# v loaded as bf16 from the GpSimd queue, and clock-sized dummy matmuls, in a fused linear-attention and feed-forward kernel

## The chip, the cores and the metric

The kernel runs on one core of one Trainium2 chip. The time is the device time of one execution in microseconds (us), and less is better. Quoted times are medians over the executions of a comparison; a run counts as slow when it is over 1.5% above the fastest of the same kernel, else as fast. Slow runs stand in the medians, but not in the ratios. The granted clock is the share of TensorE's full clock that the chip let through. The engines in the profile lines are PE (TensorE), ACT (ScalarE), DVE (VectorE), POOL (GpSimd) and SP (SyncE, which only issues DMAs here). A cast is an elementwise multiply by a decay table that also turns float32 into bf16; in this kernel most casts of q and k run on GpSimd, all the arithmetic between the two large matmuls on ScalarE and VectorE.

## The reference

Attention with a decay per head, worked out block by block with a carried state, and then two matmuls with a smooth clipped function between them.

```python
# q, k, v: (4, 8, 768, 64) float32; w_in: (512, 2048); w_out: (2048, 512); output (3072, 512)
for b in range(nb):                                   # blocks of 64 positions
    intra = einsum('bhic,bhjc->bhij', qb, kb) * Dmask[None]
    intra = einsum('bhij,bhjd->bhid', intra, vb)
    inter = einsum('bhid,bhde->bhie', qb * lam_pow[None], kv_state)
    out[:, :, sl] = intra + inter
    kv_state = lam_block * kv_state + einsum('bhsd,bhse->bhde', kb * rev_pow, vb)
# ...
h = x @ w_in                                          # x: attention output, (3072, 512)
g = where(h >= 1, h, where(h <= -1, 0, (h + 1)**2 / 4))
return g @ w_out
```

## The kernel before

The attention goes over the tokens in 12 pairs of 128-token chunks ("pair m" below, 0 to 11). For each pair q, k and v are loaded, 512 KB each in float32, by three DMAs from the SP queue. The weights are loaded by eight DMAs from GpSimd, which cast them to bf16 on the way (512 KB each as written): four blocks of w_in, four of w_out.

```python
# loads of one pair: x = 0 is q, 1 is k, 2 is v
t = ld.tile([128, H, 2, D], F32, name=f"x{x}f", tag=f"x{x}f")
i = (k, v)[x - 1][b, :, s0:s0 + 2 * C, :].rearrange("h (j e) d -> j h (e d)", e=2)
d = nc.sync.dma_start(out=t.rearrange("p h e d -> p h (e d)"), in_=i)
# ... (and then, for v, one cast for each chunk)
nc.scalar.copy(out=v_sb[c % NV], in_=qkv_ld[c, 2])
# casts of k and q; eng is VectorE for a few early chunks, else GpSimd
eng.tensor_tensor(ho(ks[c])[:, bs], hs(qkv_ld[c, 1])[:, bs], ho(_bc(tab, 2, D))[:, bs], op=AX.mult)
# between the two large matmuls, on VectorE, once for each 128x1024 piece
nc.vector.tensor_scalar(t, r, 0.5, 1.0, op0=AX.mult, op1=AX.min)
nc.vector.tensor_tensor(w, r, t, op=AX.subtract)
nc.vector.tensor_tensor(gT[s][...], w[...], t[...], op=AX.mult)
```

The order of the instructions on each engine is worked out when the kernel is built, by a planner in the kernel: each operation has a duration, needs, and a due time, and an engine takes the ready operation that is due first. Where an operation needs an earlier one on the same engine, the planner counts from the earlier one's issue, not from the end of its transfer, unless the need is entered as `gate`:

```python
ready[u.eng].append((max(y.t if y.eng == u.eng and y.key != u.gate else y.end + ...
# a weight load enters its wait as a gate
add(("w",) + it, "POOL", 900, lambda it=it, wait=gated: f_w(it, wait), need, due=pos_ * 1e-3, dma=2560)
if key is not None:
    OPS[("w",) + it].gate = key
```

While PE has nothing to do at the start, dummy matmuls (the planner's `warm`) fill it; they are meant to bring its clock up and to keep it there. In the trace of this kernel they start 0.213 us apart from 4.17 to 8.2 us and 0.109 us apart from 8.37 on; the first clock record, full clock, begins at 8.32 (the page counts the time before it as full).

## Time and profile before

| | before |
|---|---|
| median of 3 (lowest to highest) | 221.37 us (221.31 to 224.28) |
| span of the profiled execution, granted clock | 217.8 us, 0.997 |
| PE streaming of real work, without dummies | 181.0 us |
| first matmul with w_in, with w_out | 19.29 us, 40.73 us |
| ScalarE casts of v | 24, together 14.9 us |

The prediction below shows the page's main lines. Three more views are needed later. First, GpSimd by time; columns are start, length, engine, line, operation and tiles, count, and in brackets the idle time before it and what ended it.

```profile
23.74 1.55 POOL L167 DMA_DIRECT2D w_out_sb<-in_moe_w_out_dram  x2 [7.75 <-DMA w_in_sb<-in_moe_w_in_dram]
27.95 1.28 POOL L300 TENSOR_TENSOR qs<-x0f,tab_q 128x512 bf16<-128x512 f32 x1 [2.66 <-DMA x0f<-in_q_dram]
30.78 1.04 POOL L292 TENSOR_TENSOR ks<-x1f,tab_p 128x512 bf16<-128x512 f32 x1 [1.55 <-DMA x1f<-in_k_dram]
```

The two w_out loads go as soon as the third w_in block is there (23.45 us). Second, GpSimd and VectorE where both are busy:

```profile
47.34 2.42 POOL L292 TENSOR_TENSOR ks<-x1f,tab_p 128x512 bf16<-128x512 f32 x2 [4.99 <-DMA x1f<-in_k_dram]
```

### The profile page before, as it was taken

What the parts mean: (1) busy time and instruction counts of PE and PEld (TensorE: products, weight loads), DVE (VectorE), ACT (ScalarE), POOL (GpSimd) and SP (SyncE); (2) the same over time, 40 slices, a digit from 0 to 9 for tenths busy, and PEclk for the clock granted to TensorE, in tenths of its full rate; (3) what the DMA queues carried; (4) which work ended last, traced back from release to release, by engine and by line L of the source; (5) the groups of instructions that cost most, each with busy time, mean ns of one, the idle gap of its engine ahead of it and who ended that gap; (6) DMA issues with size and microseconds to landing.
All of it is one profiled execution on the core that took longest, in us unless ns stands there. A gap on an engine that the chain in (4) does not pass through costs nothing.

```text
span 217.8 us, 5513 instructions
## 1 busy us (share of the span) xinstructions
PE 206.8 (95%) x2343; PEld 120.9 (55%) x2343; DVE 148.6 (68%) x235; ACT 115.4 (53%) x200; POOL 60.2 (28%) x63
## 2 busy tenths in 40 slices
PE   3999878999999999999999999999999999999993
PEld 2777667557546767766654454544544444444442
DVE  4585975799980899899899769668467455454301
ACT  3257667427617867396557556564634643555020
POOL 5390242337382662366263421000000000000000
PEclk9999999999999999999999999999999999999998
DMA  6999999999899999999999966211011101110022
GB/s 168 290 236 196 252 235 192 203 282 176 227 236 245 219 258 170 263 230 266 181 286 207 272 192 163 38 53 48 0 51 48 43 8 48 48 48 16 35 96 96
DMA packets 64586, 34.43 MB, mean 158 GB/s; under 512 B 20402, under 2 KB 61618, under 8 KB 64562
## 3 DMA queue, kind: packets, MB, share of 16 engines
q1 hardware_dynamic: 60336, 29.89, 61.5%
q0 software_dynamic: 4224, 4.19, 11.9%
q8 instruction: 18, 0.29, 0.6%
q14 instruction: 6, 0.05, 0.1%
q10 hardware_dynamic: 2, 0.00, 0.0%
HBM read 27.26 MB, written 6.29 MB: 154 GB/s over the span
## 4 chain that ended last, share of the span: by engine, by line
PE 79%; DMA 15%; SPq 2%; ACT 1%; DVE 1%; issue 1%
PE py L487 36%; PE ph L439 34%; DMA x2f<-in_v_dram 9%; DMA x0f<-in_q_dram 3%; DMA w_in_sb<-in_moe_w_in_dram 3%; PE px L388 3%; PE ps L360 2%; PE px L372 2%; PE py L481 1%; SPq L557 1%; PE ps L401 1%; DVE sc L421 1%; ACT r L448 1%; ACT xT L428 0%; PE pt L360 0%
## 5 line engine op out<-in xcount | busy, mean ns | idle before, releaser
L439 PE MATMUL ph<-xT,w_in_sb 128*128 128x256 bf16 (+1 forms) x576 | 95.8, 308 | 2.6 <-ACT xT L428 1.1
L448 ACT ACTIVATE r<-ph,one 128x512 bf16<-128x512 f32 x96 | 65.6, 688 | 51.9 <-PE ph L439 43.7
L487 PE MATMUL py<-w_out_sb,gT 128*128 128x512 bf16 x368 | 90.6, 380 | 0.0
L439 PEld LDWEIGHTS <-w_in_sb 128*128 128x128 bf16 x576 | 54.9, 98 | 32.7 <-issue 2.1
L487 PEld LDWEIGHTS <-gT 128*128 128x128 bf16 x368 | 34.4, 98 | 38.0
L458 DVE TENSOR_SCALAR t<-r 128x1024 bf16<-128x1024 bf16 x48 | 27.6, 575 | 21.7 <-ACT r L448 21.7
L464 DVE TENSOR_TENSOR w<-r,t 128x1024 bf16<-128x1024 bf16 x48 | 40.1, 835 | 1.3
L469 DVE TENSOR_TENSOR gT<-w,t 128x1024 bf16<-128x1024 bf16 x48 | 37.7, 785 | 1.3
L300 POOL TENSOR_TENSOR qs<-x0f,tab_q 128x512 bf16<-128x512 f32 (+1 forms) x22 | 26.1, 1204 | 43.7 <-DMA x0f<-in_q_dram 33.7
L292 POOL TENSOR_TENSOR ks<-x1f,tab_p 128x512 bf16<-128x512 f32 (+1 forms) x20 | 25.4, 1285 | 14.2 <-DMA x1f<-in_k_dram 9.0
L421 DVE TENSOR_TENSOR sc<-ps,causal 128x512 bf16<-128x512 f32 x23 | 15.8, 689 | 12.4 <-PE pt L360 11.0
L492 ACT COPY osb<-py 128x512 f32<-128x512 f32 x23 | 13.5, 587 | 16.5 <-PE py L487 15.5
L428 ACT CAST xT<-px 128x512 bf16<-128x512 f32 x24 | 13.1, 587 | 13.0 <-PE px L388 9.1
L421 DVE TENSOR_TENSOR sc<-pt,causal 128x512 bf16<-128x512 f32 x22 | 14.9, 679 | 0.0
L315 ACT CAST v<-x2f 128x512 bf16<-128x512 f32 x24 | 13.8, 621 | 1.1 <-DMA x2f<-in_v_dram 1.1
L274 PE MATMUL ph<-ident 128*128 128x256 bf16 x68 | 10.8, 315 | 0.0
L360 PE MATMUL ps<-qT,kT 64*64 64x128 bf16 x184 | 10.6, 220 | 0.0
L360 PEld LDWEIGHTS <-kT 64*64 64x64 bf16 x384 | 7.7, 106 | 4.3 <-issue 4.0
L416 ACT CAST ub<-state 128x256 bf16<-128x256 f32 x19 | 7.7, 405 | 4.0 <-DVE state L407 2.0
L360 PE MATMUL pt<-qT,kT 64*64 64x128 bf16 x176 | 9.7, 219 | 0.0
L409 DVE TENSOR_TENSOR state<-state,ps 128x256 f32<-128x256 f32 x8 | 3.3, 416 | 7.8 <-PE pt L401 6.9
L388 PEld LDWEIGHTS <-v 64*64 64x64 bf16 x384 | 5.8, 106 | 4.7 <-issue 4.7
(59 smaller groups left out, 89.0 us busy)
## 6 DMA issues: line engine op xcount, KB each, us to landing
x0f<-in_q_dram SPq DMA_DIRECT2D x12, 512.0 KB, 5.8
x1f<-in_k_dram SPq DMA_DIRECT2D x12, 512.0 KB, 6.8
x2f<-in_v_dram SPq DMA_DIRECT2D x12, 512.0 KB, 7.2
out_dram<-osb SPq DMA_DIRECT2D x23, 256.0 KB, 2.1
w_in_sb<-in_moe_w_in_dram POOLq DMA_DIRECT2D x4, 512.0 KB, 8.7
w_out_sb<-in_moe_w_out_dram POOLq DMA_DIRECT2D x4, 512.0 KB, 10.8
kT<-ks SPq DMA_TRANSPOSE x18, 4.1
out_dram<-osb SPq DMA_DIRECT2D x1, 192.0 KB, 1.9
```

The lines of the kernel that those rows point to most:

```text
L292: eng.tensor_tensor(ho(ks[c])[:, bs], hs(qkv_ld[c, 1])[:, bs], ho(_bc(tab, 2, D))[:, bs], op=AX.mult)
L300: eng.tensor_tensor(ho(qs[m, e])[:, bs], hs(qkv_ld[m, 0][:, :, e])[:, bs], ho(_bc(tab_q[:, e, m % (NCB // 2), :], 2, D))[:, bs], op=AX.mult)
L315: nc.scalar.copy(out=v_sb[c % NV], in_=qkv_ld[c, 2])
L360: nc.tensor.matmul(pst[a, r][HD[i], b, :], lhsT=kT[a][HD[r], b, HD[i]], rhs=q_cols(2 * m + i, b, HD[r]), start=True, stop=True)
L421: nc.vector.tensor_tensor(sc_sb[c][:, g], pst[c, g], _bc(causal2[:, c % 2], 1, HP), op=AX.mult)
L439: nc.tensor.matmul(ph[:, j * m:(j + 1) * m], lhsT=w_in_sb[:, ko, (ni + j) * 128:(ni + j + 1) * 128], rhs=xT[s][:, ko, tok], start=(ko == 0 ...
L448: nc.scalar.activation(out=o, in_=x, func=AF.Relu, bias=one[:, 0:1])
L458: nc.vector.tensor_scalar(t, r, 0.5, 1.0, op0=AX.mult, op1=AX.min)
L464: nc.vector.tensor_tensor(w, r, t, op=AX.subtract)
L469: nc.vector.tensor_tensor(gT[s][:, f - RW * n:f, tok].rearrange("p (a b) m -> p a b m", a=RW), w.rearrange("p a (b m) -> p a b m", m=m), t ...
L487: nc.tensor.matmul(py_t[s, ms], lhsT=gT[s][:, ko, ms * 128:(ms + 1) * 128], rhs=w_out_sb[:, ko, :], start=(ko == 0), stop=(ko == FO - 1))
L492: nc.scalar.copy(out=osb[s, ms], in_=py_t[s, ms])
```

## The change

The intent is to take v's casts off ScalarE, and its loads off the SP queue, by letting a GpSimd DMA write bf16 directly. The dummy matmuls are counted at the clock that they run at (213 ns each instead of 107), so that they no longer delay the first transposes.

```diff
+    def f_loadv(m, wait):
+        i = v[b, :, s0:s0 + 2 * C, :].rearrange("h (j e) d -> j h (e d)", e=2)
+        d = nc.gpsimd.dma_start(out=v_sb[m % NV].rearrange("p h e d -> p h (e d)"), in_=i)
+        if wait is not None:
+            tc.add_manual_dep(d.ins, ld_dma[wait] if isinstance(wait, tuple) else w_dma[wait].ins.name, SYNC)
...
-    def cast_v(c):
-        nc.scalar.copy(out=v_sb[c % NV], in_=qkv_ld[c, 2])
...
+    GATE_V = {2: 3, 3: 5}     # v(2) waits for w_in block 3, v(3) for w_out block 1 (counted from 0)
...
+                add(("lv", m), "POOL", 3400 if m == 0 else VNS, ... lambda m=m, g=g: f_loadv(m, g),
+                    [key, ("C", m - NV), ("C", m - 1 - NV), ("u", m - NV)], due=pos_ * 1e-3 if m < EARLY else od - LDV, dma=VDMA)
...
-    EARLY = 3
+    EARLY = 6                 # loads of pairs below this are due at once
...
-    WARM = (2700, 18000, 107, 0.8)
+    WARM = (4200, 18000, 213, 0.8, 8300)
```

Left out here: v(0) is issued early in the set-up, pair 3 comes after the w_out blocks in the order, its q and k loads wait for one w_out block more, several leads of the planner are larger (q and k are cast and transposed further ahead), pair 4 joins the merged matmul groups, and a few k casts move between VectorE and GpSimd.

More of the change, by code (lines that the diff above doesn't have):

```diff
@@ L65 @@
     W_IN = (4, 4, 4, 4)
-    MERGED = tuple(range(5,12))
+    MERGED = tuple(range(4,12))
     SWITCH = 96
     W_OF = [i for i, n in enumerate(W_IN) for _ in range(n)]
-    ORDER = [0, 1, (0, 0), (0, 1), (0, 2), (0, 3), 2, (1, 0), (1, 1), 3, (1, 2), (1, 3)]
-    D0 = (8350, 10000, 15450, 17000)
+    ORDER = [0, 1, (0, 0), (0, 1), (0, 2), (0, 3), 2, (1, 0), (1, 1), (1, 2), (1, 3), 3]
+    D0 = (8350, 10000, 15450, 15000)
     FIRST = [(0, 2), (2, 4)]
     L0 = [(0, 0), (0, 1), (0, 2), (0, 3), (1, 0), (1, 1), (1, 2), (1, 3)]
-    GATE = {(0, 0): ('lq', 1), 2: 0, (1, 0): 2, 3: 4, (1, 2): 4}
+    GATE = {(0, 0): ('lq', 1), 2: 0, (1, 0): 2, 3: 5, (1, 2): 4}
     LORD = {}
+    GATE_V = {2: 3, 3: 5}
+    VNS, VDMA = 1800, 1350
+    LDV = 20000
+    GEN = 1350, 1800
     DBG = False
@@ L104 @@
     SYNC = mybir.DependencyInfo(mybir.DependencyClass.Sync, mybir.DependencyReason.DATA)
+    NUB, NV = 4, 4
+    v_sb = [const.tile([128, H, 2, D], BF16, name=f"v{i}") for i in range(NV)]
+    def f_loadv(m, wait):
+        b, s0 = m // (NCB // 2), 2 * (m % (NCB // 2)) * C
+        i = v[b, :, s0:s0 + 2 * C, :].rearrange("h (j e) d -> j h (e d)", e=2)
+        d = nc.gpsimd.dma_start(out=v_sb[m % NV].rearrange("p h e d -> p h (e d)"), in_=i)
+        ld_dma["lv", m] = d.ins.name
+        if wait is not None:
+            tc.add_manual_dep(d.ins, ld_dma[wait] if isinstance(wait, tuple) else w_dma[wait].ins.name, SYNC)
     nc.scalar.preload_act_table_set("natural_log_exp_and_others")
@@ L114 @@
     make_identity(nc, ident)
+    f_loadv(0, None)
     causal2 = const.tile([128, 2, 128], F32)
@@ L121 @@
                 base=base, pattern=[[1, 2], [2, 64]], channel_multiplier=-2)
-    NUB, NV = 4, 4
     ub = [const.tile([128, HP, D], BF16, name=f"ub{i}") for i in range(NUB)]
-    v_sb = [const.tile([128, H, D], BF16, name=f"v{i}") for i in range(NV)]
     state = const.tile([128, HP, D], F32)
@@ L188 @@
     LDD, STD = 16000, 3000
-    QXD, KXD = 7000, 7000
-    AD, BD = (8000, 4000), (4000, 2000)
-    UD, TD = (9000, 9000), (8000, 8000)
-    KT_ACT = (1,)
-    K_DVE = (0,1,2,3,5)
-    ON_DVE = ((0,0),(0,1),(2,1))
-    SHARED = (1,(0,1))
-    W_AFTER = {1: ("cq", 1, 0)}
+    QXD, KXD = 12000, 10000
+    AD, BD = (7000, 7000), (3000, 3500)
+    UD, TD = (12000, 9000), (12000, 8000)
+    KT_ACT = (1,3)
+    K_DVE = (0,2,3)
+    ON_DVE = ((0,0),(0,1))
+    SHARED = ()
+    W_AFTER = {1: ("cq", 1, 1)}
     def run_plan(free):
@@ L222, in run_plan @@
                 ready[x.eng].append((0, x))
-        out_seq, xfer, dma_free, fetched = [], [0] * RING, FIRST_BYTE, 0
+        out_seq, xfer, dma_free, fetched, hw_free = [], [0] * RING, FIRST_BYTE, 0, FIRST_BYTE
         while len(out_seq) < len(ops):
@@ L237, in run_plan @@
             if x.dma:
-                dma_free = max(dma_free, t + (1300 if e == "SP" else 2100)) + x.dma
-                x.end = dma_free + (400 if x.key[0] in ("lk", "lv", "lq") and x.key[1] < CPS // 2 else 1000 if x.key[:2] == ("w", 0) else 1400)
+                hw = x.key[0] in ("lk", "lq")
+                dma_free = max(dma_free, t + (1300 if e == "SP" else 2100)) + (GEN[0] if hw else x.dma)
+                if hw:
+                    hw_free = max(hw_free, t + 1300) + GEN[1]
+                x.end = max(dma_free, hw_free if hw else 0) + (400 if x.key[0] in ("lk", "lq") and x.key[1] < CPS // 2 else 1000 if x.key[:2] == ("w", 0) or x.key[0] == "lv" else 1400)
                 if x.key[0] in ("lk", "lv", "lq") and x.key[1] >= FAR // 2:
@@ L252, in run_plan @@
                 n = int((t - pe_end - 50) * WARM[3] / WARM[2])
+                w = 256 if t < WARM[4] else 512
                 if t > WARM[1]:
@@ L258, in run_plan @@
                         print(f"{t / 1e3:9.3f} 0 WARM {n} {x.key}")
-                    warm(max(n, 0))
+                    warm(max(n, 0), w)
                     if x.key in (("s", 1), ("C", 0)):
@@ L264, in run_plan, with warm @@
             x.fn()
-    WARM = (2700, 18000, 107, 0.8)
+    WARM = (4200, 18000, 213, 0.8, 8300)
     hot = [None]
-    def warm(n):
+    def warm(n, w):
         for _ in range(n):
@@ L273, in warm @@
                 hot[0] = pp_h.tile([128, MS], F32, name="ph", tag="ph")
-            nc.tensor.matmul(hot[0][:, :256], lhsT=ident, rhs=_bc(ident, 1, 2), start=True, stop=True)
+            nc.tensor.matmul(hot[0][:, :w], lhsT=ident, rhs=_bc(ident, 1, w // 128), start=True, stop=True)
     def mm(*cols):
@@ L387, in f_c @@
                     c, (r, b, _) = 2 * m + i, place(2 * j + g)
-                    nc.tensor.matmul(px[HD[g], i, j, :], lhsT=v_sb[(2 * m + e) % NV][HD[i], 2 * j + g, :],
+                    nc.tensor.matmul(px[HD[g], i, j, :], lhsT=v_sb[m % NV][HD[i], 2 * j + g, e, :],
                                      rhs=sc_sb[2 * m + e][HD[i], r, b, :],
@@ L401, in f_u @@
                         nc.tensor.matmul(pu[i][HD[r], b, :], lhsT=ks[2 * m + e][HD[i], 2 * b + r, :],
-                                         rhs=v_sb[(2 * m + e) % NV][HD[i], 4 * r + b, :],
+                                         rhs=v_sb[m % NV][HD[i], 4 * r + b, e, :],
                                          start=(e == 0 and b == 0), stop=True, skip_group_check=True)
@@ L512 @@
     T0, STEP = 22000, 1075
-    LEAD, APART = 6000, 3000
-    PARTS = {1: 2, 2: 2, 4: 1}
-    EARLY = 3
+    LEAD, APART = 2000, 3000
+    PARTS = {1: 2, 2: 2, 3: 2, 4: 1}
+    EARLY = 6
     parts = {s: [slice(p * MS // n, (p + 1) * MS // n) for p in range(n)] for s in range(NST) for n in (PARTS.get(s, 1),)}
@@ L554, in f_load @@
         else:
-            t = ld.tile([128, H, 2, D], F32, name=f"x{x}f", tag=f"x{x}f")
-            i = (k, v)[x - 1][b, :, s0:s0 + 2 * C, :].rearrange("h (j e) d -> j h (e d)", e=2)
+            t = ld.tile([128, H, 2, D], F32, name="x1f", tag="x1f")
+            i = k[b, :, s0:s0 + 2 * C, :].rearrange("h (j e) d -> j h (e d)", e=2)
             d = nc.sync.dma_start(out=t.rearrange("p h e d -> p h (e d)"), in_=i)
@@ L582 @@
             add(("w",) + it, "POOL", 900, lambda it=it, wait=gated: f_w(it, wait), need, due=pos_ * 1e-3,
-                dma=2560)
+                dma=2600)
             if key is not None:
@@ L591 @@
         for x in LORD.get(m, (0, 1, 2)):
+            if x == 2:
+                g = GATE_V.get(m)
+                key = None if g is None else g if isinstance(g, tuple) else ("w",) + w_seen[g]
+                add(("lv", m), "POOL", 3400 if m == 0 else VNS, (lambda: None) if m == 0 else lambda m=m, g=g: f_loadv(m, g),
+                    [key, ("C", m - NV), ("C", m - 1 - NV), ("u", m - NV)], due=pos_ * 1e-3 if m < EARLY else od - LDV, dma=VDMA)
+                pos_ += 1
+                continue
             need = [("w",) + w_seen[gated] if gated is not None else ("w",) + w_seen[-2] if len(w_seen) > 1 else None]
-            need += [[("cq", m - LQ, 0), ("cq", m - LQ, 1), ("cq", m - LQ, 9)], [("cast", 2 * (m - LD) + 1, 1), ("cast", 2 * (m - LD) + 1, 9)],
-                     [("cast", 2 * (m - LD) + 1, 2)]][x]
+            need += [[("cq", m - LQ, 0), ("cq", m - LQ, 1), ("cq", m - LQ, 9)], [("cast", 2 * (m - LD) + 1, 1), ("cast", 2 * (m - LD) + 1, 9)]][x]
             add(("lq lk lv".split()[x], m), "SP", 700, lambda m=m, x=x, wait=gated: f_load(2 * m, x, wait), need,
@@ L611 @@
                 [("lk", m), ("cast", c - 1, 1), ("t", c - NQK), u_op(m - NQK // 2)])
-            add(("cast", c, 2), "ACT", 640, lambda c=c: cast_v(c), [("lv", m), ("C", m - NV // 2), u_op(m - NV // 2), ("cast", c - 1, 2)])
         for i in range(2):
@@ L637 @@
                 add(("t", c), "SP", 1200, lambda c=c: f_kx(c), [("cast", c, 1), ("m", c - NQT, 1)], due=od - KXD, dma=640)
-        u_need = lambda m: [x for c in (2 * m, 2 * m + 1) for x in (("cast", c, 9), ("cast", c, 1), ("cast", c, 2))] + \
+        u_need = lambda m: [x for c in (2 * m, 2 * m + 1) for x in (("cast", c, 9), ("cast", c, 1))] + [("lv", m)] + \
             [("sum", 2 * m - 1 if m % (NCB // 2) else 2 * m - 2), ("m", 2 * m - 1, 0), ("m", 2 * m - 1, 1), ("kT", 2 * m + 1) if m != 1 else None]
@@ L656 @@
             add(("B", 0), "PE", 412, f_n0, [("ub", 0)] + qk(1), due=od - 1500, extra=FILL)
-            add(("C", 0), "PE", 640, lambda: f_c(0), [("B", 0), ("m", 0, 1), ("m", 1, 0), ("m", 1, 1), ("cast", 1, 2)], due=od, extra=FILL)
+            add(("C", 0), "PE", 640, lambda: f_c(0), [("B", 0), ("m", 0, 1), ("m", 1, 0), ("m", 1, 1), ("lv", 0)], due=od, extra=FILL)
         else:
@@ L670 @@
             add(("C", m), "PE", 448 + 240 * nxt + 2 * SWITCH, lambda m=m, nxt=nxt: (f_c(m), f_u(m + 1) if nxt else None),
-                [("B", m), ("m", c0 + 1, 0), ("m", c0 + 1, 1), ("cast", c0 + 1, 2)] + (u_need(m + 1) if nxt else []), due=od, extra=FILL)
+                [("B", m), ("m", c0 + 1, 0), ("m", c0 + 1, 1), ("lv", m)] + (u_need(m + 1) if nxt else []), due=od, extra=FILL)
         for c in (c0, c0 + 1):
@@ L723 @@
             add(("st", y), "SP", 550, lambda a=(s, ms): f_st(*a), [("y", y), ("st", y - 1)], due=st_due(y), dma=780)
-    run_plan({"PE": 4000, "ACT": 5600, "DVE": 4500, "POOL": 4300, "SP": 800})
+    run_plan({"PE": 4000, "ACT": 5600, "DVE": 4500, "POOL": 1600, "SP": 800})
 _INS = ['q', 'k', 'v', 'lam', 'moe_w_in', 'moe_w_out']
```

## The prediction

Cut from the recorded text, and marked in it, are statements on the hardware that no trace or run of this case shows. No term of its sum is among them: 2.3 + 1.6 + 0.3 = 4.2 us, from 221.4 to 217.2, and with small planner gains 217.0. Figures that it counts with, as the two traces show them: matmuls of 512 columns that follow each other start 0.216 us apart, 2.37 columns per ns, taken as 2.4; four 64x64 matmuls of 128 columns start within 0.01 us and the next four 0.053 us later, hence the quarter; a switch between 128x128 and 64x64 adds 0.09 to 0.10 us. A weight load makes 528 packets on GpSimd's DMA queue (4224 for the eight), a v load 1040 (12480 for the twelve, after).

> **What bounds the kernel now.** I read the busy shares first, then the slices, then the chain of waits in order of time, then the costliest groups and the tensor engine's own timeline.
>
> ```profile
> PE 206.8 (95%) x2343; PEld 120.9 (55%) x2343; DVE 148.6 (68%) x235; ACT 115.4 (53%) x200; POOL 60.2 (28%) x63
> ...
> PE   3999878999999999999999999999999999999993
> ...
> DMA  6999999999899999999999966211011101110022
> ```
>
> PE is the bound: nine tenths in almost every slice. But a busy PE need not be a useful PE. I added up the columns of all matmuls in the trace, dummies left out (columns / 2.4 per ns, a 64x64 tile counted as a quarter): 181.0 us of streaming, of a last matmul that ends at 214.5. So 33.5 us hold no real work. By stretches of the timeline: the first 19.3 us, before the first matmul with w_in, hold only about 3.5 us of it (15.5 lost); from there to 48 us another 7 or so are lost; from 48 to 140 some 8, mostly 0.1 us seams; 140 to 214.5 about 3. ACT and DVE have room on average, so only the first 48 us offer much.
>
> The chain of waits, in order of time, says what the first 38 us wait for:
>
> ```profile
> 3.27 7.11 DMA x0f<-in_q_dram
> 10.38 0.30 issue
> 10.69 5.72 DMA w_in_sb<-in_moe_w_in_dram
> ...
> 17.53 19.11 DMA x2f<-in_v_dram
> ...
> 37.18 0.61 ACT v L315
> ```
>
> Columns are start and length in us. It is a pure DMA chain: second q load, first w_in block, third v load (landed 36.64), then the ScalarE cast of that v, then the matmuls. After 38 us the chain is PE. The view of PE by time shows the same thing as holes:
>
> ```profile
> 27.36 1.16 PE L439 MATMUL ph<-xT,w_in_sb 128*128 128x256 bf16 x9 [0.90 <-DMA w_in_sb<-in_moe_w_in_dram]
> 29.57 3.65 PE L439 MATMUL ph<-xT,w_in_sb 128*128 128x256 bf16 x31 [1.05 <-ACT xT L428]
> ...
> 37.33 0.31 PE L401 MATMUL ps<-v,ks 64*64 64x64 bf16 x8 [0.22 <-ACT v L315]
> ```
>
> The bracket is PE's idle time and what ended it: w_in late, xT late (queued on ACT behind the work for that w_in), v late. Counting start to start, the holes are 1.1 + 1.2 us at 27 to 30, 1.6 us between 34.5 and 38.4, 0.5 at 45, 0.5 at 94: 4.9 us. These rows matter for the change:
>
> ```profile
> L315 ACT CAST v<-x2f 128x512 bf16<-128x512 f32 x24 | 13.8, 621 | 1.1 <-DMA x2f<-in_v_dram 1.1
> L274 PE MATMUL ph<-ident 128*128 128x256 bf16 x68 | 10.8, 315 | 0.0
> ...
> x2f<-in_v_dram SPq DMA_DIRECT2D x12, 512.0 KB, 7.2
> ```
>
> [...] With the SP queue alone the first six loads land 1.80 us apart (4.97, 6.77, 8.58, 10.38, 12.20, 13.97), and 4 to 12 us carries 1.17 MB per 4 us, 293 GB/s. With GpSimd's weight loads beside them, counted by the fp32 bytes they read (twice the bf16 they write), the stretches 12 to 32 us carry 350 to 380 GB/s. So the SP queue alone leaves about a fifth idle.
> [...] the 256-column dummies start 0.21 us apart from 4.17 to 8.2 and 0.11 us apart after that.
> [...]t at L458 takes 947 ns beside a GpSimd tensor op, 422 otherwise[...] the eight weight issues took 747 to 927 ns, and the two gT ops beside one averaged 680 ns against an undisturbed 670. Only two samples.
>
> **The change part by part.**
> 1. ScalarE loses 24 casts of 621 ns, 14.9 us by their sum, 13.8 as a union. ACT is 53% busy and PE hardly waits for it, so this is worth little except where a cast stands ahead of something urgent: at 16.21 two v casts hold xT until 17.25 (about 1 us), and at 37.3 and 37.8 PE waits for two (0.4 us of idle).
> 2. The 12 v loads (6.3 MB) leave the SP queue. It keeps 24 loads, the stores and transposes. At start-up two of the first six loads go. The second q load, third in its queue instead of fourth, would land at 8.58 if nothing shared, later as v(0) and v(1) share the engines: I take 9.4, 1 us earlier. The first w_in block follows. By the fourth w_in block some 7.9 MB have been read by 27.3 us; at 355 GB/s instead of the 328 they averaged since 3.2 us that is 22.3 us of transfer, so 25.6: 1.7 us earlier. By the fourth k load (47.2 us, 14.2 MB) it is 3.9 us. The third v load, at the end of the chain above, should land 3 to 4 us earlier.
> 3. GpSimd gains 12 issues. A weight issue describes 512 pieces in 0.78 us, a v load 1024, so estimate 1.6 us each, 19 us, plus about one and a half more casts (1.2 us each) from the new split. POOL goes from 60 busy us (28%, issues not counted) to perhaps 62 counted, 87 with all issues. Most of it falls before 135 us: room, but casts can queue behind an issue.
> 4. Dummies. Before, their number was worked out at 107 ns each while they ran at 213. The 23 in the first batch held PE to 8.87, although the first q cast was ready at 6.51 (5.07 + 1.44), so the first transpose started at 8.70, 2.2 us late. Planned at 213 ns they should end before it. That brings the first k transpose (10.02; its cast was done at 8.30) forward too, but then it waits for its own load: 1.3 us of the 2.2 is my guess, as v(0) slows q(0) and k(0) by 0.5 to 1 us. Fewer casts between the masks on DVE and no v casts before xT give another 1 to 2. First w_in matmul: 19.3 to about 16.5, as long as w_in's first block lands by then (16.41 now, 15.3 expected).
> 5. New leads, order of w_out and v, one more merged matmul group (two 96 ns switches): tuning that lets the planner use this; alone below 0.5 us.
>
> **The sum.** These overlap. An earlier start helps only as far as w_in keeps up, and w_in comes 1.7 us earlier; so at 27 us I count 1.7 plus the 1.2 us xT hole, of which half closes: 2.3. The holes of 34 to 46 us (2.1) close by three quarters, since v and w_out come 3 to 4 us earlier: 1.6. The hole at 94 us may close: 0.3. From 140 us on nothing changes. 4.2 us: 221.4 - 4.2 = 217.2; small planner gains bring 217.0.
>
> **Rivals.**
> (a) GpSimd becomes the wait. Before, it waited 33.7 us for q loads and never made PE wait visibly. In its in-order queue a v issue that waits for a buffer[...] could take back 1 to 3 us: 219 to 220. For it: DVE is 95% busy at 48 to 64 and 93 to 95% at 80 to 120[...]. Against it: the two gT samples, and POOL's slack.
> (b) The transfer was hidden anyway: PE at nine tenths from slice 2. Then only the dummy part counts, about 1 us: 220.3. Against it: the chain of waits is DMA down to 38 us.
> (c) Both queues run at the mixed rate and start-up is fully latency-bound: the first w_in matmul at 15.5 and all holes gone, 3 + 4: 214.5.
> (d) v beside q and k delays k(0), and the front gains nothing: 218.5.
>
> **Range and chances.** The middle is 217.0, which happens to be 2.0% below 221.37, so the first two outcomes are near equal. Low end 214.5 from (c), high end 220.3 from (a) and (b). Slower by 2% would take GpSimd starving PE for 9 us; nothing points there.
>
> **What would show it.** Right: v loads landing on the software queue, the SP loads still 1.8 us apart but two fewer; the second q load landed by 9.5; the first transpose before 7.5; first w_in matmul near 16.5; third v load landed by 33.5; the idle at 27 to 38 mostly gone; ACT near 101 us; L469 still about 785 ns. Wrong: PE idle ended by POOL or by a v DMA after 48 us; v issues much over 1.6 us;[...] k(0) landing after 8 us; or the time from 140 us to the end changed, which I hold for fixed.

## More of the kernel before

```profile
47.59 1.26 DVE L458 TENSOR_SCALAR t<-r 128x1024 bf16<-128x1024 bf16 x1
48.89 1.42 DVE L464 TENSOR_TENSOR w<-r,t 128x1024 bf16<-128x1024 bf16 x1
```

They get in each other's way, and take turns: t needs 0.42 us alone and 1.26 here, w 0.69 alone and 1.42 here, and a cast that takes 1.04 alone takes 1.2. So an overlap costs VectorE about the rest of one cast. Over all 48 operations of the group w:

```profile
L464 DVE TENSOR_TENSOR w<-r,t 128x1024 bf16<-128x1024 bf16 x48 | 40.1, 835 | 1.3
```

The numbers behind the bar are busy time in us and the mean of one in ns: 835 instead of an undisturbed 690.

## The result, and the profile after

| | before | after |
|---|---|---|
| median of 4 | 221.34 us (220.22 to 224.28) | 239.91 us (237.73 to 241.25) |
| span of the profiled execution, granted clock | 217.8 us, 0.997 | 239.5 us, 0.964 |
| first transpose | 8.70 us | 5.82 us |
| first matmul with w_in, with w_out | 19.29, 40.73 us | 17.84, 48.67 us |
| last matmul ends | 214.5 us | 236.5 us |
| real streaming of PE | 181.0 us | 181.0 us |

The change is slower by 8.5%: ratio 1.0848, 95% interval 1.073 to 1.0965. Ratios here and below are the mean time of one kernel's fast runs over that of the other's fast runs of the same rounds, so not quite the ratio of the medians. Of the four runs of the kernel before one (224.28 us) counts as slow; the other three have a mean of 220.97 us, the kernel after 239.68. The two profiled executions (219.49 and 241.25 us) lie 1.9 us below and 1.3 us above their medians, so the losses that are read from the two traces below add up to some 3 us more than the 18.6 us between the medians.

The page after, busy times, PE by slices and the granted clock by slices:

```profile
PE 208.5 (87%) x2358; PEld 125.0 (52%) x2358; DVE 153.9 (64%) x231; ACT 104.6 (44%) x177; POOL 65.7 (27%) x76
...
PE   3989720899359999979979999999999999999994
...
PEclk9999995699968999999999999999999999999999
```

ScalarE did lose its casts (115.4 us to 104.6), and POOL is still at 27% of the span. Yet PE, at seven tenths or more from the second slice on before, now has a hole in the sixth and seventh slices and another in the eleventh and twelfth (a slice is 6 us), and the clock falls in or after each. The busy shares give no hint of who did that.

To place the loss, I marked the points at which PE has done the same real work (matmul columns, without dummies, as in the prediction), and compared the times.

| same work done as before at | 48.0 us | 90.0 us | 140.1 us | the last matmul |
|---|---|---|---|---|
| after | 57.95 us | 110.5 us | 161.5 us | 236.5 us |
| lost so far | 10.0 us | 20.5 us | 21.4 us | 22.0 us |

So there are two losses of about 10 us each, one in the first 48 us of work and one in the next 42, and hardly anything later. The view of engine busy time by stretch shows both. Columns: stretch, length, then busy us and instructions of PE, its weight loads, VectorE, ScalarE and GpSimd, the granted clock, the DMA share and GB/s. The kernel after:

```profile
31.00:42.00 11.00, 0.25 (x3) 0.00 (x0) 0.00 (x0) 0.00 (x0) 2.84 (x4) 0.74 0.93 151
42.00:56.00 14.00, 13.27 (x170) 9.11 (x171) 8.22 (x16) 5.50 (x10) 4.49 (x5) 0.84 1.31 226
56.00:68.00 12.00, 6.03 (x44) 4.11 (x42) 11.93 (x3) 2.58 (x5) 10.93 (x11) 0.96 1.24 221
```

From 31 to 42 us next to nothing is computed: VectorE and ScalarE have no instruction, PE has 0.25 us, and GpSimd's four are two DMA issues and the first two of the late casts. From 56 to 68 VectorE reads 11.93 of 12.00 us busy, with three instructions. A "busy" engine here is one that waits inside an instruction. The same stretch before held 14 VectorE instructions in 8.71 us.

**The first loss** is in the chain of waits (start and length in us) and in GpSimd by time:

```profile
15.37 11.34 issue
26.73 1.35 POOL v L116 x2
28.46 1.52 POOL w_out_sb L181 x2
29.98 9.16 issue
40.92 1.08 POOL qs L318
```

```profile
26.72 1.77 POOL L116 DMA_DIRECT2D v<-in_v_dram  x2 [11.35 <-DMA w_in_sb<-in_moe_w_in_dram]
28.46 1.52 POOL L181 DMA_DIRECT2D w_out_sb<-in_moe_w_out_dram  x2
39.16 1.77 POOL L116 DMA_DIRECT2D v<-in_v_dram  x2 [9.18 <-DMA w_out_sb<-in_moe_w_out_dram]
40.92 2.07 POOL L318 TENSOR_TENSOR qs<-x0f,tab_q 128x512 bf16<-128x512 f32 x2
```

"issue" in the chain hides the wait that the second view names. The issue of v(2) waits for the fourth w_in block, which lands at 26.44, and holds GpSimd's queue for 11.35 us; so the w_out issue behind it goes at 28.46, although the block that it waits for landed at 22.66. The issue of v(3) then waits 9.18 us for the second w_out block (38.88). Behind it in the queue stand the casts of pair 2, whose q landed at 26.90 and whose k landed at 28.58. They start at 40.92; before, at 27.95. (Each of the two v lines holds two issues. By the semaphores that PE waits for, the second ones are v(4) and v(5), which wait for no weights.) PE stands still until the first transpose of that q:

```profile
42.05 0.61 PE L344 MATMUL pt<-ident,qs 128*128 128x128 bf16 x4 [10.80 <-POOL qs L318]
```

The clock falls in such a hole and stays low for some time after it: the records say 0.5 for the 10.24 us from 36.38 on, 4.6 us of them after PE's return. Around the second hole they say 0.5 for 6.83 us from 67.10 on. The two holes are 10.8 and 6.4 us long. A hole that long is not needed: in the first experiment below the clock stood at 0.5 for 3.41 us from 68.35 on, and no hole of PE in the 8 us before that was above 2.31 us.

Everything behind a waiting issue in GpSimd's queue waits too, for 11.35 and 9.18 us in this trace.

**The second loss.** GpSimd, then VectorE, by time:

```profile
56.05 0.89 POOL L116 DMA_DIRECT2D v<-in_v_dram  x1 [9.56 <-PE px L403]
56.95 2.05 POOL L318 TENSOR_TENSOR qs<-x0f,tab_q 128x512 bf16<-128x512 f32 x2
...
64.95 2.03 POOL L318 TENSOR_TENSOR qs<-x0f,tab_q 128x512 bf16<-128x512 f32 x2
```

```profile
55.90 0.42 DVE L473 TENSOR_SCALAR t<-r 128x1024 bf16<-128x1024 bf16 x1
56.36 11.18 DVE L479 TENSOR_TENSOR w<-r,t 128x1024 bf16<-128x1024 bf16 x1
```

The issue of v(6) waits for a buffer, and ten casts queue up behind it. A VectorE operation of 0.69 us starts while GpSimd issues v(6) (56.05 to 56.94), at 56.36, and ends at 67.54, 0.56 us after the last of the ten casts (66.98). It did not get its turn after one cast, as in the kernel before; and the casts ran 1.00 us apart, as if alone. Two shorter cases follow: 4.53 us at 99.97, behind an issue and four casts, and 7.07 us at 114.84, behind an issue and six. The second hole of PE is this wait, seen through ScalarE, which needed the buffer that VectorE held:

```profile
68.39 3.57 PE L454 MATMUL ph<-xT,w_in_sb 128*128 128x256 bf16 x16 [6.36 <-ACT r L463]
```

In the groups it is the one row that stands out, against the 835 ns above:

```profile
L479 DVE TENSOR_TENSOR w<-r,t 128x1024 bf16<-128x1024 bf16 x48 | 51.1, 1065 | 1.3
```

### The profile page after: what moved, and what is told of

It reads as the page before. It is cut to its first block, busy times and chain, and to the rows that moved or that the text cites. A ratio compares the mean times of both kernels' runs of the same rounds, so it can differ in the third digit from the quotient of the medians.

```text
span 239.5 us, 5515 instructions
## 1 busy us (share of the span) xinstructions
PE 208.5 (87%) x2358; PEld 125.0 (52%) x2358; DVE 153.9 (64%) x231; ACT 104.6 (44%) x177; POOL 65.7 (27%) x76
## 4 chain that ended last, share of the span: by engine, by line
PE 64%; DVE 16%; issue 9%; POOL 4%; DMA 3%; ACT 1%; SPq 0%; ACTq 0%; POOLq 0%
PE py L502 29%; PE ph L454 26%; DVE w L479 9%; DMA x0f<-in_q_dram 3%; DVE t L473 3%; DVE sc L436 2%; PE ps L375 2%; PE px L403 2%; DVE gT L484 2%; POOL qs L318 1%; POOL w_in_sb L177 1%; PE px L387 1%; PE py L496 1%; POOL v L116 1%; PE ps L416 1%
## 5 line engine op out<-in xcount | busy, mean ns | idle before, releaser
L454 PE MATMUL ph<-xT,w_in_sb 128*128 128x256 bf16 (+1 forms) x640 | 97.7, 300 | 9.5 <-ACT r L463 7.8
L454 PEld LDWEIGHTS <-w_in_sb 128*128 128x128 bf16 x640 | 62.2, 100 | 36.9 <-issue 9.3
L479 DVE TENSOR_TENSOR w<-r,t 128x1024 bf16<-128x1024 bf16 x48 | 51.1, 1065 | 1.3
L473 DVE TENSOR_SCALAR t<-r 128x1024 bf16<-128x1024 bf16 x48 | 28.1, 585 | 21.4 <-ACT r L463 21.4
L484 DVE TENSOR_TENSOR gT<-w,t 128x1024 bf16<-128x1024 bf16 x48 | 34.6, 721 | 1.2
L310 POOL TENSOR_TENSOR ks<-x1f,tab_p 128x512 bf16<-128x512 f32 x21 | 24.0, 1161 | 35.4 <-PE pt L416 16.7
L116 POOL DMA_DIRECT2D v<-in_v_dram x12 | 11.1, 926 | 54.8 <-PE pt L416 21.0
L318 POOL TENSOR_TENSOR qs<-x0f,tab_q 128x512 bf16<-128x512 f32 x22 | 22.4, 1042 | 0.1
L351 DVE COPY kT<-pt 128x512 bf16<-128x512 bf16 x4 | 1.6, 420 | 18.1 <-PE pt L337 18.1
L344 PE MATMUL pt<-ident,qs 128*128 128x128 bf16 x8 | 1.2, 311 | 10.8 <-POOL qs L318 10.8
L344 PEld LDWEIGHTS <-qs 128*128 128x128 bf16 x24 | 2.1, 122 | 14.7 <-POOL qs L318 11.1
```

The costliest lines, as they stand in the source:

```text
L116: d = nc.gpsimd.dma_start(out=v_sb[m % NV].rearrange("p h e d -> p h (e d)"), in_=i)
L318: eng.tensor_tensor(ho(qs[m, e])[:, bs], hs(qkv_ld[m, 0][:, :, e])[:, bs], ho(_bc(tab_q[:, e, m % (NCB // 2), :], 2, D))[:, bs], op=AX.mult)
L454: nc.tensor.matmul(ph[:, j * m:(j + 1) * m], lhsT=w_in_sb[:, ko, (ni + j) * 128:(ni + j + 1) * 128], rhs=xT[s][:, ko, tok], start=(ko == 0 ...
L484: nc.vector.tensor_tensor(gT[s][:, f - RW * n:f, tok].rearrange("p (a b) m -> p a b m", a=RW), w.rearrange("p a (b m) -> p a b m", m=m), t ...
```

## The experiments

Theory Q (queue): v issues that wait stand ahead of casts in GpSimd's in-order queue. Theory L (lock-out): a VectorE operation that starts during a GpSimd DMA issue with casts directly behind it waits for all of these casts. The rival is that v from GpSimd costs too much as such, by issue time, casts moved to GpSimd, or slower transfers. Eleven kernels ran, on three chips, each chip with its own runs of the kernel before (medians 220.53, 220.74 and 221.45 us). All outputs were correct. "Lost" gives the same marks as above.

### Casts ahead of the waiting issues

Only GpSimd's order changes: the v loads from pair 3 on are put behind the casts of pair 2.

```diff
-                    [key, ("C", m - NV), ("C", m - 1 - NV), ("u", m - NV)], due=...
+                    [key, ("C", m - NV), ("C", m - 1 - NV), ("u", m - NV), ("cast", 5, 1) if m > 2 else None], due=...
```

> The changed kernel, with one edit: in GpSimd's instruction order the v loads of pairs 3, 4 and 5 come after the four casts of pair 2. Theory (a v issue that waits for a weight transfer stands in GpSimd's in-order queue ahead of casts whose data has landed): the q cast of pair 2 starts near 30 us instead of 40.9, the PE hole of 11.0 us before 42.05 shrinks below 3 us, the half clock that follows it (36.4 to 46.6) goes, and the time falls from 239.9 to about 226. The long VectorE instructions (11.2, 4.5, 7.1 us) may stay. Rival (the casts are late because their data or the engines are, or w_out is the bound): the hole stays above 8 us and the time within 2% of 239.9.

Measured: 224.4 us, ratio to before 1.0186 (1.0101 to 1.0271): still slower, and whether by 2% is unclear. GpSimd by time, to be read against the four lines of the kernel after:

```profile
27.01 0.89 POOL L116 DMA_DIRECT2D v<-in_v_dram  x1 [11.40 <-DMA w_in_sb<-in_moe_w_in_dram]
27.89 1.51 POOL L181 DMA_DIRECT2D w_out_sb<-in_moe_w_out_dram  x2
29.39 2.07 POOL L318 TENSOR_TENSOR qs<-x0f,tab_q 128x512 bf16<-128x512 f32 x2
```

The casts start at 29.39 instead of 40.92. Lost at the four marks: -0.4, 5.5, 4.6 and 5.2 us. The first loss is gone altogether, and half of the second, because the backlog of ten casts no longer forms; the longest VectorE operation is 3.30 us (at 29.45, behind a w_out issue). So one need in the planner takes the loss from 8.5% to 1.9%. What is left lies between 64 and 72 us: PE waits for transposes, and the DMA transpose of q stands in the SP queue behind two k loads that held SP for 7 us (the larger leads at work), with half clock again from 68.35.

### A pause between the issue and the casts

From pair 6 on, the first GpSimd cast after a v issue waits for the landing of that v. This makes GpSimd later, not earlier; it only parts the issue from the casts.

```diff
+        if m >= 6:
+            ld_dma["pause"] = d.ins.name
+    def pause(i, eng):
+        if eng is nc.gpsimd and "pause" in ld_dma:
+            tc.add_manual_dep(i.ins, ld_dma.pop("pause"), SYNC)
...
-        eng.tensor_tensor(...)
+        pause(eng.tensor_tensor(...), eng)
```

> The changed kernel, with one edit: from pair 6 on, the first GpSimd cast after a v issue waits until that v load has landed, so GpSimd is idle for 5 us or so between the issue and the casts. Theory [...]: no VectorE instruction over 2 us, the w group (L479 there) back from a mean of 1065 ns to 700 to 850 ns; the hole before 42 us stays; time 229 to 237. Rival (it is the length of the run of ready casts, however it starts): runs of 4 to 10 casts still occur and VectorE instructions of 4 us and more stay.

Measured: 231.62 us, ratio 1.0496 (1.0425 to 1.0566). Lost: 11.1, 13.0, 12.0, 12.7 us. The first loss stays, as it should, and the second shrinks from 10.5 to 1.9 us. No VectorE operation is longer than 1.5 us, and the mean of w is below that of the kernel before:

```profile
L485 DVE TENSOR_TENSOR w<-r,t 128x1024 bf16<-128x1024 bf16 x48 | 39.2, 817 | 1.3
```

Ten casts still run without a break, from 64.23 to 75.99 us, so the length of a run alone is not the cause. Number of issues, of casts and of transfers are those of the kernel after, which speaks against the rival.

### A GpSimd DMA issue ahead of the casts, and behind them

The counter-test adds the suspected pattern to the kernel before: from pair 3 on, a small GpSimd load with a cast (1024 pieces, its data unused) directly ahead of the first q cast of each pair, waiting for the same q load. The control has the same load, directly behind the pair's last k cast.

```diff
+        if m >= 3 and e == 0:                     # in the q cast, ahead of it; the control: in the k cast, behind it
+            src = q[b, :, s0:s0 + 2 * C, :].rearrange("h (j e) d -> j h e d", e=2)[:, :, 0]
+            d = nc.gpsimd.dma_start(out=lead_sb, in_=src)
+            tc.add_manual_dep(d.ins, ld_dma["lq", m], SYNC)
```

> The kernel before, with one addition: from pair 3 on a small GpSimd load with a cast (1024 pieces, 0.25 MB read) is issued just ahead of the first q cast of each pair, waiting for the same q load. Theory [...]: VectorE instructions of 3 us and more appear, the w group (L464 in the kernel before) rises from 835 to over 950 ns, the time from 221.3 to 224 to 232. Rival (run length alone): VectorE as before, at most 1.5 us each, time within 1% of 221.3.

> Control for the small GpSimd load of leaddma: the same load, the same bytes, once per pair from pair 3 on, but issued behind the last k cast of the pair instead of ahead of its first q cast. Theory [...]: few or no VectorE instructions over 2 us, time 221 to 224. Rival (the added traffic or GpSimd's time is what cost leaddma its 3.5%): time near 228 as there.

Ahead: 228.36 us, ratio 1.0354 (1.0286 to 1.0422), lost -0.1, 7.7, 9.2, 9.2 us. Behind: 222.74 us, one of four runs slow and left out of the ratio, 1.0059 (0.9977 to 1.0141), lost -0.1, 0.7, 1.3, 1.3 us. GpSimd and VectorE near 61 us, with the load ahead:

```profile
60.92 0.94 POOL L302 DMA_DIRECT2D lead<-in_q_dram  x1 [4.92 <-DMA x0f<-in_q_dram]
61.88 2.05 POOL L306 TENSOR_TENSOR qs<-x0f,tab_q 128x512 bf16<-128x512 f32 x2
63.89 2.03 POOL L293 TENSOR_TENSOR ks<-x1f,tab_p 128x512 bf16<-128x512 f32 x2
```

```profile
61.19 5.02 DVE L464 TENSOR_SCALAR t<-r 128x1024 bf16<-128x1024 bf16 x1
```

And with the load behind:

```profile
60.02 2.49 POOL L307 TENSOR_TENSOR qs<-x0f,tab_q 128x512 bf16<-128x512 f32 x2 [3.27 <-issue]
62.47 2.49 POOL L293 TENSOR_TENSOR ks<-x1f,tab_p 128x512 bf16<-128x512 f32 x2
64.90 0.94 POOL L298 DMA_DIRECT2D lead<-in_q_dram  x1
```

```profile
60.17 1.43 DVE L471 TENSOR_TENSOR w<-r,t 128x1024 bf16<-128x1024 bf16 x1
61.64 1.42 DVE L476 TENSOR_TENSOR gT<-w,t 128x1024 bf16<-128x1024 bf16 x1
```

The four casts are the same. With the load ahead, VectorE waits for all of them and they run 1.00 us apart; with it behind, VectorE takes turns and they run 1.22 us apart. The same bytes in the same number of DMAs cost 3.5% or 0.6% (the latter not told from zero), by their place in the queue. Theory L is shown as an effect. The mean of w was expected above 950 ns with the load ahead; it rose to 895 only, since the long waits fell on t and gT as well (gT 885 ns). Nor does every long wait cost time: in the trace with the load ahead nothing was lost up to the mark at 60.0 us (-0.1 us), although a w had taken 5.39 us at 51.16; at the mark at 64.0 us, behind the t shown above, 5.4 us were lost. I also counted it: in the kernel after and six experiments (one of these in a slow profile), 19 t, w or gT operations started during a GpSimd DMA issue with casts directly behind it, or within 0.1 us of its end. 15 ended after the last of these casts, one after the last but one, and 3 ran at normal length and were over before the first cast began or within 0.1 us of that. An operation that came later in a run of casts took 2.1 us at most.

### The dummies alone

The kernel before with the new `WARM` and the wider dummies only.

> The kernel before with the new dummy matmuls alone. My prediction: the first transpose of q starts near 6.6 instead of 8.70, the first matmul with w_in 0.5 to 1.3 us earlier than 19.29, time 220.0 to 221.0. Rival: the start-up is held by loads and casts, nothing moves by more than 0.3 us. Second rival: with fewer dummies the clock comes up later and the time rises by 0.5 to 2 us.

Measured: 220.89 us, within the expected range, but the kernel before had 220.53 on this chip: ratio 1.0012 (0.9938 to 1.0087), no gain. The first transpose comes at 5.89 us instead of 8.70 (6.6 expected). The first w_in matmul comes at 18.40 us instead of 19.29, but PE is idle for 0.90 us ahead of it, and for 1.28 us ahead of 26.96, waiting for w_in: the rest of the gain is lost to the weights' arrival. The later clock of the second rival shows in the kernel after, which has the same `WARM`: its first clock record, full clock, begins at 12.48 us, before at 8.32. What that costs was not measured by itself.

### v loads after the casts, no waits on weights

The kernel after, with `GATE_V = {}`, v(2) behind the last w_in issue, and v(m) behind the casts of pair max(2, m-3).

> The changed kernel with GpSimd's order mended throughout: no v issue waits for a weight transfer (v of pair 2 simply follows the fourth w_in block in the queue), and v of pair m from 3 on comes after the casts of pair max(2, m-3). Theory (three waits of v issues stood ahead of ready work): w_out issued near 23 us instead of 27.9, the casts of pair 3 before 50 us instead of 52.1 in castsfirst, PE holes at 42 to 47 and at 64 to 70 below 1 us each, time 218 to 222. Rival (the front-loaded loads of pairs 3 to 5 fill the DMA engines until 57 us, so order cannot help): the hole near 66 us stays above 3 us, time 223 to 226.

A miss: 226.67 us, ratio 1.0273 (1.0205 to 1.0341), not 218 to 222. w_out is issued at 24.15 and the first 48 us are fine (lost -0.8), but at the 90 us mark 7.5 us are lost. An issue behind the casts of one pair is ahead of those of the next, so the pattern came back: VectorE waited 3.08 us at 71.36 and 4.13 at 98.80, both behind a v issue. The clock stood at 0.5 for 6.83 us from 67.97 on, though PE's holes between 62 and 72 us were 1.55 us at most (under 1 us expected, above 3 us by the rival). The larger leads probably cost as well (not tested alone); the transpose of pair 3's q on the SP queue stood behind loads of pairs 4 and 5:

```profile
54.68 5.74 SPq L358 DMA_TRANSPOSE qT<-qs  x1
```

### v from GpSimd where nothing is lost by it, and for all pairs

The first is the kernel before with the new dummies, and only v(0) to v(2) from GpSimd, each into its own bf16 tile, v(2) behind the fourth w_in issue; the other nine stay as they were. The second has all twelve from GpSimd that way.

```diff
+    VSW = (0, 1, 2)            # second kernel: tuple(range(12))
+    v_pair = {m: const.tile([128, H, 2, D], BF16, name=f"vp{m}") for m in VSW}
+            if x == 2 and m in VSW:
+                add(("lv", m), "POOL", 3400 if m == 0 else 1000, ... lambda m=m: f_loadv(m),
+                    [("w", 0, 3) if m == 2 else None], due=pos_ * 1e-3, dma=1350)
```

> The kernel before with the new dummies and only the v loads of pairs 0, 1 and 2 issued from GpSimd with the cast; pairs 3 to 11 load v from SP and cast on ScalarE as before, and all other leads are those of before. Theory (the gain that I predicted exists at the start, and what lost it is v issues in GpSimd's queue later on): first matmul with w_in near 18, v of pair 2 landed by 31 instead of 36.6, holes of 34 to 38.5 us (1.6 us) mostly gone, no VectorE instruction over 2 us, time 217 to 219.5. Rival (start-up is bound by the weight transfers): holes stay, time 220 to 221.5.

> As hybrid, but all twelve v loads from GpSimd with the cast, each into its own tile, so that no issue waits for a buffer; v of pair m (4 and on) is issued behind the casts of pair m-2. Theory (it is waits and position in GpSimd's queue that cost, not the number of v issues): within 1% of hybrid, with a few VectorE instructions of 2 to 4 us where a v issue happens to stand ahead of ready casts. Rival [...]: 224 or more.

The first ran in 219.3 us (218.78 to 219.73), ratio 0.993 (0.988 to 0.9981): 0.7% faster than before, the fastest of all, within 2%. No VectorE operation is above 1.53 us. The first w_in matmul came at 17.83 us (near 18 expected), and of the holes from 34 to 38.5 us one of 0.20 us is left. PE's two longest waits between 20 and 48 us are for w_in and, after that, for xT:

```profile
27.43 1.92 PE L452 MATMUL ph<-xT,w_in_sb 128*128 128x256 bf16 x16 [1.72 <-DMA w_in_sb<-in_moe_w_in_dram]
31.10 2.89 PE L452 MATMUL ph<-xT,w_in_sb 128*128 128x256 bf16 x24 [1.18 <-ACT xT L441]
```

The fourth w_in block landed at 27.39 us (before: 27.32), so v's move did not bring the weights forward; v(2) landed at 31.12, while the chain of waits before had v's third load at 36.64. The profiled execution (218.0 us) is not shorter than that of before (217.8), so where the 0.7% lies can't be read from these two traces.

The second is a miss: 231.75 us, ratio 1.046 (1.0379 to 1.0542) on its fast runs, where I had expected the time of the first within 1%. I had overlooked that v(m) would stand ahead of the next pair's casts. Its profile fell in the slow state, so I take from it only that the pattern is there: an issue at 64.30 with four casts behind, and a w of 5.18 us at 64.67. The same kernel's casts of pair 3's k started at 47.73 us, as in the kernel before (47.34).

### q and k of pair 2 later

The first of the two again, with the loads of pair 2's q and k held until the second, or the third, w_in block has landed instead of the first (`GATE` of 2: 1, or 2), to let w_in through.

> hybrid with one edit: the q and k loads of pair 2 wait for the second w_in block instead of the first, so that they share the DMA engines with fewer w_in blocks. Theory (the holes of 1.9 us at 27 and 1.3 us at 31 us in hybrid wait for the fourth w_in block, which shares the engines with q and k): that block lands about 1 us earlier than 27.3, the two holes together shrink by about 1 us, time 218 to 219. Rival (q and k of pair 2 are then late themselves): PE waits for casts near 33 us, time as hybrid or more.

> As hybrid_g1, with the q and k loads of pair 2 behind the third w_in block. Theory: fourth w_in block 1.5 to 2 us earlier than in hybrid, but q and k of pair 2 land near 30 to 31 us; time 217.5 to 219.5. Rival as there, likelier: 220 or more.

Both missed their times: 222.23 us (218 to 219 expected), ratio 1.0044 (1.0001 to 1.0087), and 219.82 us (217.5 to 219.5 expected), ratio 0.9945 (0.9901 to 0.9989). With the third block, the last w_in block landed at 26.04, 1.35 us earlier, and no time was gained over 0.993. With the second, it landed at 26.97 (0.42 us earlier instead of 1), and k(2) landed late enough for two w_out issues to stand directly ahead of four casts, and a w took 4.56 us at 39.98. So weight loads lock VectorE out as v loads do, if casts stand behind them; the 3.30 us in the first experiment is a second case.

### The kernel after, mended

The kernel after with both causes treated: `GATE_V = {}`, v(m) behind the casts of pair max(2, m-1), the pause from pair 3 on, q and k loads from pair 5 on, and the stores, behind transposes.

> The changed kernel with all three suspected costs taken out: no v issue waits for a weight transfer, v of pair m comes behind the casts of the pair before (and the stores and the q and k loads of pair 5 and later behind the transposes of earlier pairs, so that loads are not front-loaded), and from pair 3 on the first GpSimd cast after a v issue waits for that v. Theory (queue order, lock-out and front-loading are all of the loss): no VectorE instruction over 2 us, PE holes of more than 1 us only where w_in is awaited before 30 us, time 217 to 221. Rival (v through GpSimd for all pairs costs something else, such as slower q and k loads beside it): 223 or more without such holes being explained by the three.

Measured: 222.91 us over six runs, one of them slow and left out of the ratio, 1.006 (0.9996 to 1.0124). That is outside the expected 217 to 221 us; of the chip's eleven runs of the kernel before (median 221.45) three were slow. No VectorE operation is above 1.58 us, and the mean of w is 767 ns. PE still waits 1.35 us for masks at 64.23, and the clock is at 0.5 for 3.41 us from 66.49 on; none of the three mended costs accounts for that, and its cause is open. (About 30 matmul records are missing from this trace, so no marks are given.) All twelve v loads still come from GpSimd and no cast went back to ScalarE: 8.5% became 0.6%. The rival, that moving v costs this much as such, is out; nor is there a gain.

## Why the prediction was wrong

The prediction was 217.0 us, 214.5 to 220.3; the change took 239.91.

**The step that failed** is part 3 of the change: "room, but casts can queue behind an issue". It sized GpSimd's share by duration, 12 issues of an estimated 1.6 us. They took 0.93 us each; even less. What cost the time was what an issue waits for and what stands behind it. Rival (a) named this, "a v issue that waits for a buffer", and gave it 1 to 3 us. It measured 10.0 us by the first mark for waits on weights. No run was needed to see that: the diff has v(2) wait for the fourth w_in block and v(3) for the second w_out block, these landed at 27.32 and 36.27 us before, and `EARLY = 6` makes v(3) due at once, ahead of casts that ran at 27.95. The line "Slower by 2% would take GpSimd starving PE for 9 us; nothing points there" skipped that look. The planner's missing `gate` explains why it chose this order; that was not tested by itself.

**A term that the sum lacked** is the lock-out, the second 10.5 us, with the half clock that followed it. I had judged how GpSimd disturbs VectorE from t beside a cast (947 ns instead of 422) and from gT beside an issue, "the two gT ops beside one averaged 680 ns", and counted the latter against rival (a). They were the wrong samples: in the kernel before no issue after 20 us has casts directly behind it. The two losses are not independent. Mending the queue alone removed 6.6 of the 8.5 points, and the pause alone 3.5; together that is more than 8.5, as the backlog of the first made the longest run of casts for the second.

**Part 2, the transfers**, was too hopeful. The second q load landed at 9.96 us (9.4 predicted, 10.38 before), the fourth w_in block at 26.44 (25.6 predicted, 27.32 before). The stretches 4 to 8 and 8 to 12 us moved 1.29 and 1.23 MB, 323 and 307 GB/s, in which v's 512-byte reads run beside the SP queue. I had used 355, from stretches with the 2 KB weight reads, and had read from these that the SP queue alone leaves a fifth idle. That reading was wrong: from 16 to 20 us of the kernel before, the SP queue moved next to nothing and the weight reads alone carried 1.48 MB, 370 GB/s. The higher rate goes with those reads, not with two queues side by side: v's reads from GpSimd beside the SP queue brought 5 to 10% over the 293 GB/s of the SP queue alone. v(2) landed at 31.19, "landed by 33.5" holds.

**Part 4, the dummies**: the first transpose came at 5.82 us, as promised before 7.5. The first w_in matmul came at 17.84, not 16.5, although its block was there at 15.88. By the trace, the masks of pair 0 on VectorE stood behind a cast of pair 1's k, which waited for that k's landing at 13.02; the mask ended at 15.26, the attention matmul began at 15.59, and the second xT cast ended at 17.79. Alone, the dummies were worth nothing that the runs can tell from zero, nearest rival (b), which gave them 1 us.

**Part 1** held: ScalarE fell from 115.4 to 104.6 us (101 predicted), and it was worth little. **Part 5**, "tuning ... alone below 0.5 us", was too low, as far as is known: the larger leads filled the SP queue with loads ahead of transposes, and that is where the loss is left with the casts first (5.9 us between the first two marks). The lock-out of 3.30 us in that run lies before the first mark, where nothing is lost, and no later VectorE operation took more than 1.70 us. The leads weren't tested by themselves.

**"From 140 us on nothing changes"** held: from that mark to the end the kernel after took 0.6 us longer. gT's mean was 721 ns instead of the expected 785.

**Open**: why VectorE does not get its turn between casts that follow an issue directly. The runs show when it happens, not how.

## What to carry to other kernels

When a DMA issue moves to another engine's queue, don't add up issue times: write down, for each one, what it waits for, when that landed in the old trace, and which instructions stand behind it. Keep GpSimd DMA issues from standing directly ahead of GpSimd work that VectorE has to take turns with (here casts: 1.26 us instead of 0.42 for a t beside one): the same DMAs cost 3.5% ahead of the casts and 0.6%, not told from zero, behind them, and a pause after the issue cut the second loss from 10.5 to 1.9 us. And read a "busy" engine with a few very long instructions as a waiting one (here VectorE, 11.93 of 12.00 us in three instructions).
